# Linear attention, 32 heads: the second head's k on ScalarE's DMA queue, and a new order of the first two heads

## The chip, the core and the metric

The kernel runs on one core of a Trainium2 chip. The metric is the device time of one execution in microseconds (us). Work is spread over TensorE (PE; its weight loads are shown as PEld), VectorE (DVE), ScalarE (ACT) and GpSimd (POOL); SyncE (SP) issues the DMAs. Each of these runs its own list of instructions in order and waits on semaphores for the others.

## The reference

q, k and v are bf16, 1 x 32 heads x 2048 rows x 128 columns; the output has the same shape.

```python
def reference(q, k, v):
    phi_q = jnp.where(q > 0, q + 1, jnp.exp(q)) + 1e-6
    phi_k = jnp.where(k > 0, k + 1, jnp.exp(k)) + 1e-6
    kv = jnp.einsum("bhsd,bhse->bhde", phi_k, v)
    z = jnp.einsum("bhsd->bhd", phi_k)
    num = jnp.einsum("bhqd,bhde->bhqe", phi_q, kv)
    den = jnp.einsum("bhqd,bhd->bhq", phi_q, z)[..., None] + 1e-6
    return num / den
```

The kernel writes phi(x) as the sum of two parts, min(exp(x), 1) + 1e-6 and max(x, 0), and multiplies by each part in its own matmul. z comes out of the same matmuls as kv, as a column of ones beside v.

## The kernel before

A head is 16 tiles of 128 rows. Per head h, the operations are these. The number after the dot is a part of the head (halves, for the first head's k, v and q), and the line is that of the profile of before.

- SP, L324: ldk, ldq, ldv load the head's k, q and v, 512 KB each, into one of 7 buffers; L418: st stores the result.
- ACT, L336: ek = exp(k). L372: eq = exp of q transposed, read from PSUM. L378: rqa = relu of the first 8 tiles of q transposed. L362: kvs copies kv from PSUM to SBUF.
- DVE, L339: em finishes exp(k). L342: rkd = max(k, 0) for half the tiles. L374: emq finishes exp(q). L381: rqb = max(q, 0) for the tiles that rqa leaves. L403 and L410: r and f, reciprocal of the denominator and division.
- POOL, L350: v1 copies v beside the column of ones. L346: rkp = max(k, 0) for the other tiles.
- PE, L368: T transposes q into the PSUM tile xT. L357: kv, 32 matmuls for kv and z of the head, accumulated in one PSUM tile. L389, L394, L396: n, numerator and denominator. L315: w1, w2 and w0 are matmuls on the identity whose result nobody reads (4, 4 and 15 of them).

There is one xT and one kv tile in PSUM. So T of head h+1 waits for eq, rqa and rqb of head h, and kv of head h+1 waits for kvs of head h. ek and em write one of two buffers, which is free again when kv two heads earlier is through.

Nothing is scheduled at run time: for every engine the order is a list written out by hand (ORDER), and the program derives from it which semaphores each operation waits for. Before the change the lists begin like this:

```python
"PE":  w1 w2 T0.1 T0.0 w0 T1.0 kv0.0 kv0.1 kv1.0 kv1.1 n0.0 n0.1 T2.0 ...
"DVE": eps0 ones rkd0.0 v1ones1 v1ones0 eps2 rkd1.0 em0.0 rqb0.0 emq0.0 emq0.1 em0.1 em1.0 rqb1.0 ...
"ACT": ek0.0 ek0.1 eq0.1 eq0.0 rqa0 ek1.0 eq1.0 kvs0 ek2.0 rqa1 kvs1 ek3.0 eq2.0 ...
"POOL": ident0 ident v10.0 rkp0.0 v10.1 rkp1.0 v11.0 rkp2.0 ...
"SP":  ldk0.0 ldq0.0 ldk1.0 ldv0.0 ldq1.0 ldv1.0 ldk2.0 ...
```

From the third head on, the same round repeats. The loads run ahead of the work as far as the 7 buffers and the DMA queue allow.

Of the kernel before, what the change touches and what calls it, by code (L numbers as in the profile page):

```python
# [4 lines left out]
ACT = mybir.ActivationFunctionType  # L5
ALU = mybir.AluOpType
P = 128
EPS = 1e-6
ENGINES = ("PE", "DVE", "ACT", "POOL", "SP")
NH = 32  # L10
NI, NO, NE, NR, NV, NQ, NK = 7, 12, 2, 2, 2, 2, 2
WARM = (15, 4, 4)
HALVES = ((0, 8), (8, 16))
# [14 lines left out]
def q_parts(h):  # L28
    return HALVES if h == 0 else ((0, 8), (8, 12), (12, 16)) if h == NH - 1 else WHOLE

# [17 lines left out]
def na(h):  # L48
    return NA[h]


def groups(h):
    if h == NH - 1:
        return ((0, 2, 3, 0), (6, 2, 3, 2), (12, 2, 2, 4))
    return ((0, 4, 3, 0), (12, 2, 2, 4))


def st_parts(h):
    return ((0, 6), (6, 12), (12, 16)) if h == NH - 1 else WHOLE

# [10 lines left out]
def t_parts(h):  # L71
    return HALVES if h in (0, NH - 1) else WHOLE


def rqb_parts(h):
    if na(h) == 16:
        return ()
    if h == NH - 1:
        return tuple(p for p in q_parts(h) if p[0] >= na(h))
# [2 lines left out]

ORDER = {
    "PE": """
        w1 w2 T0.1 T0.0 w0 T1.0 kv0.0 kv0.1 kv1.0 kv1.1 n0.0 n0.1 T2.0 kv2.0 kv2.1 n1.0 T3.0 n1.1 kv3.0 kv3.1 n2.0
        T4.0 n2.1 kv4.0 kv4.1 n3.0 T5.0 n3.1 kv5.0 kv5.1 n4.0 T6.0 n4.1 kv6.0 kv6.1 n5.0 T7.0 n5.1 kv7.0 kv7.1 n6.0
        T8.0 n6.1 kv8.0 kv8.1 n7.0 T9.0 n7.1 kv9.0 kv9.1 n8.0 T10.0 n8.1 kv10.0 kv10.1 n9.0 T11.0 n9.1 kv11.0 kv11.1
        n10.0 T12.0 n10.1 kv12.0 kv12.1 n11.0 T13.0 n11.1 kv13.0 kv13.1 n12.0 T14.0 n12.1 kv14.0 kv14.1 n13.0 T15.0
# [5 lines left out]
        n30.0 n30.1 n31.0 n31.1 n31.2  # L94
    """,
    "DVE": """
        eps0 ones rkd0.0 v1ones1 v1ones0 eps2 rkd1.0 em0.0 rqb0.0 emq0.0 emq0.1 em0.1 em1.0 rqb1.0 rkd2.0 eps1
        emq1.0 rkd3.0 r0.0 em2.0 f0.0 em3.0 rqb2.0 r0.1 emq2.0 f0.1 r1.0 rkd4.0 f1.0 em4.0 rqb3.0 r1.1 rkd5.0 f1.1
        r2.0 emq3.0 f2.0 em5.0 rqb4.0 r2.1 rkd6.0 f2.1 r3.0 emq4.0 f3.0 em6.0 rqb5.0 r3.1 rkd7.0 f3.1 r4.0 emq5.0
        f4.0 em7.0 rqb6.0 r4.1 rkd8.0 f4.1 r5.0 emq6.0 f5.0 em8.0 rqb7.0 r5.1 rkd9.0 f5.1 r6.0 emq7.0 f6.0 em9.0  # L100
# [12 lines left out]
        emq31.0 r29.1 f29.1 r30.0 f30.0 r30.1 f30.1 emq31.2 r31.0 f31.0 r31.1 r31.2 f31.1 f31.2  # L113
    """,
    "ACT": """
        ek0.0 ek0.1 eq0.1 eq0.0 rqa0 ek1.0 eq1.0 kvs0 ek2.0 rqa1 kvs1 ek3.0 eq2.0 kvs2 rqa2 ek4.0 eq3.0 kvs3 rqa3
        ek5.0 eq4.0 kvs4 rqa4 ek6.0 eq5.0 kvs5 rqa5 ek7.0 eq6.0 kvs6 rqa6 ek8.0 eq7.0 kvs7 rqa7 ek9.0 eq8.0 kvs8
        rqa8 ek10.0 eq9.0 kvs9 rqa9 ek11.0 eq10.0 kvs10 rqa10 ek12.0 eq11.0 kvs11 rqa11 ek13.0 eq12.0 kvs12 rqa12
        ek14.0 eq13.0 kvs13 rqa13 ek15.0 eq14.0 kvs14 rqa14 ek16.0 eq15.0 kvs15 rqa15 ek17.0 eq16.0 kvs16 rqa16
# [10 lines left out]
        v128.0 rkp28.0 v129.0 rkp29.0 v130.0 rkp30.0 v131.0 rkp31.0  # L130
    """,
    "SP": """
        ldk0.0 ldq0.0 ldk1.0 ldv0.0 ldq1.0 ldv1.0 ldk2.0 ldk3.0 ldv2.0 ldq2.0 ldv3.0 ldq3.0 ldk4.0 ldv4.0 ldk5.0
        ldq4.0 ldv5.0 ldk6.0 ldq5.0 ldq6.0 ldv6.0 ldk7.0 ldq7.0 ldk8.0 st0.0 ldv7.0 ldv8.0 ldv9.0 ldk9.0 ldk10.0
        ldq8.0 ldk11.0 ldq9.0 st1.0 ldv10.0 ldq10.0 ldq11.0 ldk12.0 ldk13.0 ldv11.0 ldv12.0 ldq12.0 st2.0 ldv13.0
        ldk14.0 ldk15.0 ldv14.0 ldq13.0 ldq14.0 st3.0 ldq15.0 ldq16.0 ldk16.0 ldv15.0 ldq17.0 st4.0 ldv16.0 ldk17.0
# [19 lines left out]
class Program:  # L156
# [10 lines left out]
    def add(self, eng, key, fn, deps=(), dma=None, inc=True):  # L167
        assert key not in self.op, key
        self.op[key] = (eng, fn, tuple(deps), dma, inc)
# [71 lines left out]
def bass_standalone__linear_attn_elu__prompt_kernel(nc: bass.Bass, q: bass.AP, k: bass.AP, v: bass.AP, out: bass.AP):  # L241
    B, H, S, D = q.shape
    assert D == P and S == 16 * P and B * H == NH
    NT = S // P
# [6 lines left out]
    rows = lambda t, h: t[h].rearrange("(p j) d -> p j d", j=NT)  # L251

    with ExitStack() as es:
        names = [0]

        def alloc(make, shape, dt):
            names[0] += 1
            return es.enter_context(make(f"la_{names[0]}", shape, dt))
# [5 lines left out]
        sb = lambda shape, dt=bf16: alloc(nc.sbuf_tensor, shape, dt)  # L264
# [5 lines left out]
        rden_sb = sb([P, 2, NT], fp32)  # L270
        o_sb = sb([P, NO, NT, D])
        ident, ones, epsr = sb([P, P]), sb([P, P]), sb([P, 3])
        xT = alloc(nc.psum_tensor, [P, NT, P], bf16)
        o_ps = alloc(nc.psum_tensor, [P, 6 * 512], fp32)
        KV0 = 5 * 512 + 2 * NC
# [3 lines left out]
        add = pr.add  # L279
# [26 lines left out]
        add("DVE", "eps1", lambda g: g.memset(epsr[0:1, :], eb), ["eps0"])  # L306
        add("DVE", "eps2", lambda g: g.memset(epsr[32:33, :], ec), ["eps0"])
        add("DVE", "ones", lambda g: g.memset(ones[:], 1.0))
        for s in range(NV):
            add("DVE", f"v1ones{s}", lambda g, s=s: g.memset(v1_sb[:, s, :, D:D + 2], 1.0))  # L310

# [9 lines left out]
            warm(f"w{i}", n)  # L321

        def load(name, dst, src, h, i, t0, t1, last):
            add("SP", f"ld{name}{h}.{i}", lambda e: e.dma_start(dst[:, h % NI, t0:t1], rows(src, h)[:, t0:t1]),  # L324
                last, dma=f"{name}{h % NI}.{i}")

        def head(h):
            for i, (a, b) in enumerate(ld_parts(h)):
                load("k", k_sb, kf, h, i, a, b, freed(NI, h, ("ek", k_parts), ("rkd", rkd_parts), ("rkp", rkp_parts)))
            for i, (a, b) in enumerate(ld_parts(h)):  # L330
                load("q", q_sb, qf, h, i, a, b, freed(NI, h, ("T", t_parts)))
            for i, (a, b) in enumerate(ld_parts(h)):
                load("v", v_sb, vf, h, i, a, b, freed(NI, h, ("v1", v_parts)))
# [130 lines left out]
```

## Time and profile before

| | |
|---|---|
| median of 7 runs | 170.62 us (169.57 to 171.11) |
| the profiled execution | 170.46 us, of which span 169.1 us |
| mean granted TensorE clock | 0.995 |
| busy: PE, PEld, DVE, ACT, POOL | 158.5, 153.1, 154.2, 153.7, 85.3 us |
| DMA | 67.53 MB, mean 399 GB/s over the span |

The span is the time from the first to the last instruction of the profile, and the rest of the 170.46 us lies around it. Matmuls overlap, so the pitch of a group of matmuls (from its start to the start of the next group) says more than its busy time. A timeline row gives the start, the busy time, the engine and line, the operation with its tiles and how many instructions were merged; in brackets stands how long the engine had been idle and what ended that. Rows of one engine may overlap by some 0.1 us, since the next instruction starts before the last has written everything.

The lines in 40 slices show how full the engines are over the span:

```profile
DVE  1297799999999999999999999999999989999990
ACT  3999899999999999999999999999999999995800
POOL 1089546645566545655566554655456553535000
DMA  5999999999999999999999999999999999999984
```

### The profile page before, as it was taken

Reading aid. Unit: us, or ns where it says so; the run is one execution under the profiler, and the core shown is the slowest. Engines: PE = TensorE matmul, PEld = TensorE weight load, DVE = VectorE, ACT = ScalarE, POOL = GpSimd, SP = SyncE. Lnnn points to the kernel's source line nnn. Section 1 sums busy time; section 2 is a strip of 40 time slices with the busy share of each in tenths; the row PEclk is TensorE's granted clock in tenths of the full one; section 3 lists DMA queues with packets and bytes.
Section 4 is the critical chain, followed back from the end, with each engine's and each line's share of the span. In section 5 each row is a group of like instructions: output and inputs, shape, how many; then the busy total and the mean of one; then the engine's idle time right before and its main releaser. Section 6 shows DMA issues by size and latency. Waiting matters only on the chain.

```text
span 169.1 us, 6305 instructions
## 1 busy us (share of the span) xinstructions
PE 158.5 (94%) x2775; PEld 153.1 (91%) x2775; DVE 154.2 (91%) x267; ACT 153.7 (91%) x133; POOL 85.3 (50%) x71
## 2 busy tenths in 40 slices
PE   6997999999999999999999999999999999999750
PEld 2576999999999999999999999999999999999740
DVE  1297799999999999999999999999999989999990
ACT  3999899999999999999999999999999999995800
POOL 1089546645566545655566554655456553535000
PEclk9999999999999999999999999999999999999998
DMA  5999999999999999999999999999999999999984
GB/s 208 390 420 412 407 410 406 410 419 405 406 415 412 418 407 412 413 414 418 412 415 418 412 421 413 411 420 415 418 417 414 423 411 418 416 413 418 395 330 169
DMA packets 18748, 67.53 MB, mean 399 GB/s; under 512 B 2080, under 2 KB 2464, under 8 KB 18720
## 3 DMA queue, kind: packets, MB, share of 16 engines
q1 hardware_dynamic: 18720, 67.12, 98.5%
q8 instruction: 22, 0.36, 0.8%
q14 instruction: 6, 0.05, 0.1%
HBM read 50.33 MB, written 16.78 MB: 397 GB/s over the span
## 4 chain that ended last, share of the span: by engine, by line
ACT 46%; PE 17%; DVE 14%; DMA 13%; SPq 3%; POOL 3%; issue 1%; DVEq 0%
ACT la L372 18%; ACT la L336 17%; DMA la<-in_q_dram 9%; ACT la L378 9%; DVE la L410 8%; PE la L357 7%; DMA la<-in_v_dram 4%; PE la L394 4%; PE la L368 3%; PE la L396 3%; SPq L324 2%; ACT la L362 2%; DVE la L381 2%; DVE la L374 2%; POOL la L350 2%; POOL la L346 1%
## 5 line engine op out<-in xcount | busy, mean ns | idle before, releaser
L410 DVE TENSOR_TENSOR la<-la 128x1536 bf16<-128x1536 f32 (+2 forms) x65 | 77.6, 1195 | 0.3
L396 PE MATMUL la<-la 128*128 128x129 bf16 x512 | 67.7, 219 | 0.0
L394 PE MATMUL la<-la 128*128 128x129 bf16 x512 | 67.7, 218 | 0.0
L357 PE MATMUL la<-la 128*128 128x129 bf16 x1024 | 63.3, 220 | 1.2 <-POOL la L350 1.2
L350 POOL COPY la<-la 128x1024 int32<-128x1024 int32 (+1 forms) x33 | 40.3, 1221 | 46.3 <-DVE la L403 27.7
L372 ACT ACTIVATE la<-la 128x2048 bf16<-128x2048 bf16 (+2 forms) x35 | 60.4, 1730 | 3.5 <-PE la L396 2.0
L336 ACT ACTIVATE la<-la 128x2048 bf16<-128x2048 bf16 (+1 forms) x33 | 61.3, 1859 | 2.0 <-DMA la<-in_k_dram 2.0
L357 PEld LDWEIGHTS la<-la 128*128 128x128 bf16 x1024 | 59.3, 98 | 1.3 <-DVE la L381 1.3
L346 POOL TENSOR_SCALAR la<-la 128x1024 bf16<-128x1024 bf16 x32 | 44.5, 1390 | 22.9 <-DVE la L410 22.9
L396 PEld LDWEIGHTS la<-la 128*128 128x128 bf16 x512 | 49.3, 96 | 0.0
L394 PEld LDWEIGHTS la<-la 128*128 128x128 bf16 x512 | 47.0, 97 | 0.0
L368 PE MATMUL la<-la 128*128 128x128 bf16 x512 | 34.5, 222 | 0.7 <-DMA la<-in_q_dram 0.6
L389 PE MATMUL la<-la 128*128 128x3 bf16 (+1 forms) x192 | 32.4, 169 | 1.6 <-DVE la L410 1.6
L378 ACT ACTIVATE la<-la 128x1024 bf16<-128x1024 bf16 (+1 forms) x32 | 33.5, 1046 | 0.0
L368 PEld LDWEIGHTS la<-la 128*128 128x128 bf16 x512 | 29.8, 99 | 2.4 <-DMA la<-in_q_dram 1.2
L339 DVE TENSOR_SCALAR la<-la 128x2048 bf16<-128x2048 bf16 (+1 forms) x33 | 23.0, 700 | 0.0
L374 DVE TENSOR_SCALAR la<-la 128x2048 bf16<-128x2048 bf16 (+2 forms) x35 | 22.6, 650 | 0.0
L381 DVE TENSOR_SCALAR la<-la 128x1024 bf16<-128x1024 bf16 x31 | 21.0, 678 | 1.5 <-ACT la L372 1.2
L342 DVE TENSOR_SCALAR la<-la 128x1024 bf16<-128x1024 bf16 x32 | 14.9, 466 | 6.4 <-DMA la<-in_k_dram 6.0
L389 PEld LDWEIGHTS la<-la 128*128 128x128 bf16 x192 | 18.7, 97 | 2.1 <-DVE la L410 1.8
L403 DVE RECIPROCAL la<-la 128x12 f32<-128x12 f32 (+2 forms) x65 | 12.7, 197 | 1.9 <-PE la L396 1.0
L362 ACT ACTIVATE la<-la 128x129 bf16<-128x129 f32 x32 | 9.0, 282 | 0.5 <-PE la L357 0.5
(14 smaller groups left out, 11.8 us busy)
## 6 DMA issues: line engine op xcount, KB each, us to landing
la<-in_k_dram SPq DMA_DIRECT2D x32, 512.0 KB, 15.6
la<-in_q_dram SPq DMA_DIRECT2D x32, 512.0 KB, 15.6
la<-in_v_dram SPq DMA_DIRECT2D x32, 512.0 KB, 15.2
out_dram<-la SPq DMA_DIRECT2D x31, 512.0 KB, 15.5
out_dram<-la SPq DMA_DIRECT2D x2, 192.0 KB, 2.8
out_dram<-la SPq DMA_DIRECT2D x1, 128.0 KB, 3.9
```

Source lines behind the costliest of these rows:

```text
L336: add("ACT", f"ek{h}.{i}", lambda e, a=a, b=b: e.activation(em_sb[:, h % NE, a:b], k_sb[:, h % NI, a:b], ACT.Exp), over("ldk", h, ld_parts ...
L346: add("POOL", f"rkp{h}.{i}", lambda e, a=a, b=b: e.tensor_scalar(rk_sb[:, h % NR, a:b], k_sb[:, h % NI, a:b], BIG, 0.0, op0=ALU.min, op1=A ...
L350: add("POOL", f"v1{h}.{i}", lambda e, a=a, b=b: e.tensor_copy(v1_sb[:, h % NV, a:b, 0:D].bitcast(i32), v_sb[:, h % NI, a:b].bitcast(i32)), ...
L357: ins = e.matmul(kv_ps, lhsT=src[:, j], rhs=v1_sb[:, h % NV, j, 0:NC], start=(j + part == 0), stop=(j == NT - 1 and part == 1))
L368: ins = e.transpose(xT[:, j], q_sb[:, h % NI, j], ident[:])
L372: add("ACT", f"eq{h}.{i}", lambda e, a=a, b=b: e.activation(emq_sb[:, h % NQ, a:b], xT[:, a:b], ACT.Exp), over("T", h, t_parts, a, b) + fr ...
L374: add("DVE", f"emq{h}.{i}", lambda e, a=a, b=b: e.tensor_scalar(emq_sb[:, h % NQ, a:b], emq_sb[:, h % NQ, a:b], 1.0, EPS, op0=ALU.min, op1 ...
L378: add("ACT", f"rqa{h}", lambda e: e.activation(rq_sb[:, h % NQ, 0:n], xT[:, 0:n], ACT.Relu), over("T", h, t_parts, 0, n) + freed(NQ, h, (" ...
L389: e.matmul(_ap(o_ps[:, :], o + D, [[NC, m]]), lhsT=ones[:], rhs=epsr[:, 0:m], start=True, stop=False, skip_group_check=True)
L394: e.matmul(to, lhsT=emq_sb[:, h % NQ, t], rhs=kvs_sb[:, h % NK, 0:NC], start=False, stop=False, skip_group_check=True)
L396: ins = e.matmul(to, lhsT=rq_sb[:, h % NQ, t], rhs=kvs_sb[:, h % NK, 0:NC], start=False, stop=True, skip_group_check=True)
L410: return e.tensor_tensor(out=_ap(o_sb[:, :, :, :], first(o_sb[:, h % NO, t0, 0:1]) - first(o_sb[:, :, :, :]), [[m * D, nb], [D, m], [1, D] ...
```

## The change

Four edits, all in the first two heads:

- ldk1.0, the load of the second head's k, is taken out of SP's list and issued by ACT, on ACT's own DMA queue. In SP's list ldv0.0 now follows ldq0.0 directly.
- ACT's list begins with a new operation `exp`, an exponential of one column of the tile of ones into a small tile of its own, and then ldk1.0. `exp` waits for `ones` (DVE).
- On ACT ek1.0 moves ahead of eq0.1, eq0.0 and rqa0. On DVE em0.1 and em1.0 move ahead of rqb0.0, emq0.0 and emq0.1.
- On PE kv0.0 and kv0.1 move ahead of T1.0.

```diff
+BY_ACT = ('ldk1.0',)
...
     "PE": """
-        w1 w2 T0.1 T0.0 w0 T1.0 kv0.0 kv0.1 kv1.0 kv1.1 n0.0 n0.1 T2.0 kv2.0 kv2.1 n1.0 T3.0 n1.1 kv3.0 kv3.1 n2.0
+        w1 w2 T0.1 T0.0 w0 kv0.0 kv0.1 T1.0 kv1.0 kv1.1 n0.0 n0.1 T2.0 kv2.0 kv2.1 n1.0 T3.0 n1.1 kv3.0 kv3.1 n2.0
...
     "DVE": """
-        eps0 ones rkd0.0 v1ones1 v1ones0 eps2 rkd1.0 em0.0 rqb0.0 emq0.0 emq0.1 em0.1 em1.0 rqb1.0 rkd2.0 eps1
+        eps0 ones rkd0.0 v1ones1 v1ones0 eps2 rkd1.0 em0.0 em0.1 em1.0 rqb0.0 emq0.0 emq0.1 rqb1.0 rkd2.0 eps1
...
     "ACT": """
-        ek0.0 ek0.1 eq0.1 eq0.0 rqa0 ek1.0 eq1.0 kvs0 ek2.0 rqa1 kvs1 ek3.0 eq2.0 kvs2 rqa2 ek4.0 eq3.0 kvs3 rqa3
+        exp ldk1.0 ek0.0 ek0.1 ek1.0 eq0.1 eq0.0 rqa0 eq1.0 kvs0 ek2.0 rqa1 kvs1 ek3.0 eq2.0 kvs2 rqa2 ek4.0 eq3.0 kvs3 rqa3
...
     "SP": """
-        ldk0.0 ldq0.0 ldk1.0 ldv0.0 ldq1.0 ldv1.0 ldk2.0 ldk3.0 ldv2.0 ldq2.0 ldv3.0 ldq3.0 ldk4.0 ldv4.0 ldk5.0
+        ldk0.0 ldq0.0 ldv0.0 ldq1.0 ldv1.0 ldk2.0 ldk3.0 ldv2.0 ldq2.0 ldv3.0 ldq3.0 ldk4.0 ldv4.0 ldk5.0
...
+        first_sb = sb([P, 2])
...
+        add("ACT", "exp", lambda e: e.activation(first_sb[:, 0:1], ones[:, 0:1], ACT.Exp), ["ones"])
...
         def load(name, dst, src, h, i, t0, t1, last):
-            add("SP", f"ld{name}{h}.{i}", lambda e: e.dma_start(dst[:, h % NI, t0:t1], rows(src, h)[:, t0:t1]),
+            add("ACT" if f"ld{name}{h}.{i}" in BY_ACT else "SP", f"ld{name}{h}.{i}", lambda e: e.dma_start(dst[:, h % NI, t0:t1], rows(src, h)[:, t0:t1]),
                 last, dma=f"{name}{h % NI}.{i}")
```

## The prediction

> **What bounds the kernel now.** I read the page first: the engines' shares and the chain that ended last.
>
> ```profile
> PE 158.5 (94%) x2775; PEld 153.1 (91%) x2775; DVE 154.2 (91%) x267; ACT 153.7 (91%) x133; POOL 85.3 (50%) x71
> ACT 46%; PE 17%; DVE 14%; DMA 13%; SPq 3%; POOL 3%; issue 1%; DVEq 0%
> ```
>
> Three engines and the DMA stand near full, so the next view is busy time by stretch (columns: length, then PE, weight loads, DVE, ACT, POOL, the PE clock, the DMA share, GB/s).
>
> ```profile
> 20.00:40.00 20.00, 20.00 (x370) 19.94 (x368) 19.47 (x35) 20.00 (x19) 11.16 (x9) 1.00 1.03 409
> 80.00:100.00 20.00, 20.00 (x368) 19.83 (x366) 19.97 (x34) 20.00 (x18) 12.23 (x9) 1.00 1.02 415
> 120.00:140.00 20.00, 19.75 (x363) 19.53 (x361) 19.44 (x35) 19.70 (x18) 11.18 (x9) 1.00 1.03 416
> ```
>
> ACT is busy without a gap from 20 us on. The chain gives its round as eq 1.77, kvs 0.22, rqa 0.91, ek 1.80: 4.70 us a head. So a shift of ACT at 20 us goes through to the end, except where ACT later idles for something that does not shift, a load. The waits after 20 us and ACT's late rows show how much that is:
>
> ```profile
> PE la L368 <- DMA la<-in_q_dram: 0.2, 1, 0.2
> 137.16 1.88 ACT L372 ACTIVATE la<-la 128x2048 bf16<-128x2048 bf16 x1 [0.30 <-PE la L396]
> 155.96 1.51 ACT L372 ACTIVATE la<-la 128x512 bf16<-128x512 bf16 x2 [1.69 <-PE la L396]
> ```
>
> T27 waited 0.2 us for its q, and the exp behind it 0.30: at most 0.30 can be absorbed. The 1.69 belongs to PE's own order in the last head and moves with everything else. What the change is worth is therefore read in the first 20 us. Timelines of ACT, then PE, then DVE and POOL there (start, busy, engine and line; in brackets the idle time before and what ended it):
>
> ```profile
> 3.97 2.00 ACT L336 ACTIVATE la<-la 128x1024 bf16<-128x1024 bf16 x2 [1.96 <-DMA la<-in_k_dram]
> 6.35 1.94 ACT L372 ACTIVATE la<-la 128x1024 bf16<-128x1024 bf16 x2 [0.37 <-PE la L368]
> 9.07 1.92 ACT L336 ACTIVATE la<-la 128x2048 bf16<-128x2048 bf16 x1
> 11.35 1.88 ACT L372 ACTIVATE la<-la 128x2048 bf16<-128x2048 bf16 x1 [0.35 <-PE la L368]
> 13.16 0.28 ACT L362 ACTIVATE la<-la 128x129 bf16<-128x129 f32 x1
> 19.16 1.88 ACT L372 ACTIVATE la<-la 128x2048 bf16<-128x2048 bf16 x1 [0.78 <-PE la L368]
> ```
>
> ```profile
> 1.52 3.38 PE L315 MATMUL la<-la 128*128 128x480 bf16 x8 [1.52 <-POOL la L301]
> 5.28 1.87 PE L368 MATMUL la<-la 128*128 128x128 bf16 x16 [0.37 <-DMA la<-in_q_dram]
> 6.96 3.23 PE L315 MATMUL la<-la 128*128 128x480 bf16 x15
> 10.26 1.05 PE L368 MATMUL la<-la 128*128 128x128 bf16 x16
> 11.15 1.98 PE L357 MATMUL la<-la 128*128 128x129 bf16 x32
> 14.30 1.97 PE L357 MATMUL la<-la 128*128 128x129 bf16 x32 [1.17 <-POOL la L350]
> ```
>
> ```profile
> 7.64 0.43 DVE L342 TENSOR_SCALAR la<-la 128x1024 bf16<-128x1024 bf16 x1 [3.04 <-DMA la<-in_k_dram]
> 8.95 0.85 POOL L350 COPY la<-la 128x512 int32<-128x512 int32 x1 [7.48 <-DMA la<-in_v_dram]
> 9.77 1.21 POOL L346 TENSOR_SCALAR la<-la 128x1024 bf16<-128x1024 bf16 x1
> 10.93 0.80 POOL L350 COPY la<-la 128x512 int32<-128x512 int32 x1
> 13.12 1.03 POOL L350 COPY la<-la 128x1024 int32<-128x1024 int32 x1
> ```
>
> The names, in order. ACT: ek0, eq0, ek1, eq1, kvs0, eq2. PE: w1 w2, T0, the filler w0, T1, kv0, kv1. The four first transfers land at 3.97 (k0), 5.28 (q0), 7.64 (k1), 8.95 (v0). ACT's only idle between 3.97 and 19.16 is 0.37, 0.35, a 0.16 before kvs1, and 0.78: 1.66 us is all that a better prologue could win.
>
> **The change, part by part.**
>
> *ldk1 on ACT's queue.* One issue less on SP (0.42 us each), where v0 goes out at about 1.64 instead of 2.11. That wins nothing: issues run ahead of landings by 3.2 us at k0 and 6.8 at v0, so the transfers wait for the DMA engines. On ACT the issue takes as long (no row of ACT; SP's are 0.38 to 0.47), while ACT idles until 3.97. Cost nothing; without that idle, 0.4.
>
> When does k1 join? ACT's issue goes out between 0.74 (when SP's first does, if it need not wait for the engine) and 2.3 (table load until 2.01, and an exp of one column no longer than the 0.28 of kvs). A transfer's step is 1.31 us (3.97 to 5.28), so k0's service began by 2.66, at most 1.9 after its issue: k1 joins between 2.7, or less, and 4.2, just when q0's turn comes at 3.97. Before, q0 stood ahead of k1; now they share. The bounds for q0: 5.28, if it is still served first, and 7.64, the landing of the third transfer before, if it becomes third. Joining at 4.2 with equal shares would give 6.4, and the long third step (2.36 against 1.31) comes on top. I take 7.64, the row for "three transfers are through". v0 remains fourth, 8.95: the same four have to land by then.
>
> [...] No row of before shows two queues of loads.
>
> *`exp`.* One activation of a column, at most 0.28, in idle time before 3.97. It shifts no table load: that stands at 0.73 already. Nothing.
>
> *ek1 ahead of eq0.* ek1 (1.80) can follow ek0 as soon as k1 is there; eq0, rqa0 and rqb0 come later. Nothing is lost by that in itself: eq0 would start at 9 to 10, rqa0 end at 12.4 and T1, which needs them, is later still (below). If k0 shares with k1 too, ek0 slips by up to 1.3; the same cover hides it. On DVE, em0 and em1 ahead of rqb0 and emq0 keep the same instructions; rkd1 waits for a k1 that lands no later. Nothing.
>
> *kv0 ahead of T1 on PE.* This is the price. T1 no longer stands right behind w0. kv0.0 needs v10.0 and kv0.1 needs v10.1, POOL's copies of v0 (8.95 to 9.77, and 10.93 to 11.73). Behind T1 hangs eq1, and behind eq1 on ACT stands kvs0, which frees the one PSUM tile that kv1 writes: kv1 now waits for eq1 as well. And xT is one buffer, so eq1 cannot start from anything else.
>
> Sum with q0 at 7.64, by pitches of the rows: T0 at 7.65; w0 1.68 later (5.28 to 6.96) at 9.33; kv0 3.30 later (6.96 to 10.26) at 12.63, after v10.1 at 11.73; T1 after kv0's 1.81 (32 matmuls in the chain) at 14.44; eq1 1.09 later (10.26 to 11.35) at 15.53 instead of 11.35; kvs0 1.81 later at 17.34; kv1 after its 0.28 and a 0.03 handover at 17.65 instead of 14.30: **3.35 late**. From kv1 the order is the old one: eq2 starts 4.86 after kv1 (14.30 to 19.16), at 22.5, and ACT's own sequence (1.81 + 0.18 + 1.79 + 0.90 + 0.17 + 1.80 = 6.65 after eq1, 22.18) gets there sooner. ACT, DVE and PE leave the prologue 3.35 late, 0.30 is taken back at T27: +3.05. On the profiled execution (170.46, of which span 169.1) that is 173.5; the median of the runs lies 0.16 above it: **173.7**.
>
> *The filler's clock.* w1 and w2 ran 0.42 a matmul (3.38 / 8), w0 0.215 (3.23 / 15), on the same shape: TensorE's faster pace came at about 7 us, after an idle of only 0.37. Now PE may idle from 4.90 to 7.65. Bounds: 0 (w0 at 0.215) and 15 x 0.205 = 3.1 (all of w0 at 0.42). I take 0 in the sum, w0's own row being the nearest, and keep 3.1 for the range.
>
> [...]
>
> **Rivals.**
>
> *q0 is not held up.* k1 joins too late and lands third at 7.64. For it: the later bound of joining, 4.2. Against it: the earlier one, and that an equal share already costs q0. Then w0 ends at 10.26, kv0.0 runs, kv0.1 waits for v10.1 until 11.75, T1 at 12.66, eq1 at 13.75, kv1 at 15.87: +1.57, less 0.30: 171.9. If the long third step vanished too and v0 came 1.05 sooner, w0 would set kv0 (10.26), eq1 13.16, kv1 15.28: +0.98 less 0.30, 171.3.
>
> *The filler runs slow.* All of the 3.1 on top: 176.8; half of it 175.2. For it: the idle of 2.7 us where there was 0.37.
>
> *The shift is swallowed, no slower.* The DMA, at a share of 1.02 or more and with a 15.34 us queue for T27's q in the chain, sets the end, and the engines only wait less for loads: 170.6. It decides if engines on the path waited for loads after 20 us by at least the shift. The waits give 0.2 for PE and 0.30 for ACT; POOL's waits for v are longer, but POOL is half idle. A gain would need eq2 before 19.16, so kv1 before 14.30, so eq1 by 12.18; even with v0 in time w0 and kv0 put it at 13.16.
>
> **How the numbers follow.** Forecast 0.52, its own range 172.6 to 174.8 (q0 at 6.5 to 7.64, some of w0 slow). q0 not held up 0.22; slow filler 0.18; swallowed 0.05; something unforeseen 0.03. The range 171.7 to 175.6 leaves out the swallowed case, the cheapest of the first rival, and the worst of the slow filler. About 0.5%, 0.85 us, is what a measurement of this kernel tells from no change. Same: the swallowed case and the 171.3 corner, 0.08; faster 0.03; slower 0.89.
>
> **What would show it.** In the profile of the changed kernel T0 starts at 6.4 to 7.65 (5.28 if the first rival holds), w0 at 3.2 us in all (more if the filler is slow), T1 behind kv0 at about 14.4, eq1 near 15.5 with an ACT idle of 2 to 3 us before it, kv1 near 17.6 released by kvs0 and not by POOL, POOL's first copy still at about 8.95, and from there a 4.70 round as before. I am wrong if POOL's first copy starts near 6.5, if eq1 starts before 12.5, or if ACT shows idle time after 25 us that takes the shift back.

## The result, and the profile after

| | before | after |
|---|---|---|
| median | 170.43 us (31 runs, 169.57 to 171.28) | 172.52 us (12 runs, 171.68 to 175.16) |
| the profiled execution, and its span | 170.46, 169.1 us | 171.75, 170.2 us |

The ratio is 1.0142, with a 95% interval of 1.0114 to 1.0169; a ratio leaves out runs more than 1.5% above the fastest of their kernel, here the two longest of the twelve, and in the table of experiments below one run each of three kernels and four of twelve of the last. The kernel is slower, and 172.5 lies inside the range on record, 1.2 below the forecast. The profiled execution is among the fastest of the twelve, so the traces are compared first, and the scatter of the runs afterwards.

The first 20 us, in the same views as before: ACT (with ACT's own DMA issue), PE, then DVE and POOL. Lines of the changed kernel lie 3 higher: L339 is ek, L375 eq, L365 kvs, L371 T, L318 the filler, L360 kv, L353 v1.

```profile
1.07 0.40 ACTq L327 DMA_DIRECT2D la<-in_k_dram  x1
3.95 3.86 ACT L339 ACTIVATE la<-la 128x1024 bf16<-128x1024 bf16 x3 [1.72 <-DMA la<-in_k_dram]
7.71 1.92 ACT L375 ACTIVATE la<-la 128x1024 bf16<-128x1024 bf16 x2
14.67 1.88 ACT L375 ACTIVATE la<-la 128x2048 bf16<-128x2048 bf16 x1 [4.12 <-PE la L371]
21.65 1.88 ACT L375 ACTIVATE la<-la 128x2048 bf16<-128x2048 bf16 x1 [0.27 <-PE la L371]
```

```profile
6.56 1.89 PE L371 MATMUL la<-la 128*128 128x128 bf16 x16 [1.65 <-DMA la<-in_q_dram]
8.24 3.69 PE L318 MATMUL la<-la 128*128 128x480 bf16 x15
11.76 1.98 PE L360 MATMUL la<-la 128*128 128x129 bf16 x32
13.57 1.06 PE L371 MATMUL la<-la 128*128 128x128 bf16 x16
16.77 1.02 PE L360 MATMUL la<-la 128*128 128x129 bf16 x15 [2.14 <-ACT la L365]
```

```profile
5.90 0.43 DVE L345 TENSOR_SCALAR la<-la 128x1024 bf16<-128x1024 bf16 x1 [1.33 <-DMA la<-in_k_dram]
7.85 1.15 POOL L353 COPY la<-la 128x512 int32<-128x512 int32 x1 [6.39 <-DMA la<-in_v_dram]
```

ek0.0, ek0.1 and ek1 run without a gap (the x3 row), as the change means them to. Then ACT is idle for 4.12 us: eq1 waits for T1, T1 stands behind kv0, kv0 behind the filler, and T0 behind a q that lands third. kv1 starts at 16.77 instead of 14.30, released by kvs0 and no longer by POOL; eq2 is 2.49 late.

The end of both kernels: the two last divisions on DVE (L410 is L413 after), then SP's own wait for the stores (total, times, longest).

```profile
163.60 1.54 DVE L410 TENSOR_TENSOR la<-la 128x768 bf16<-128x768 f32 x2
SPq L435 <- DMA out_dram<-la: 3.2, 2, 2.2
```

```profile
166.49 1.55 DVE L413 TENSOR_TENSOR la<-la 128x768 bf16<-128x768 f32 x2
SPq L438 <- DMA out_dram<-la: 1.4, 2, 0.9
```

The work ends at 165.14 before and at 168.04 after, **2.9 later**. But the span ends 4.0 after the work before, and only 2.2 after it in the changed kernel. The tail gives 1.8 back, and the span is 1.1 longer.

### The profile page after: what moved, and what is told of

Read it like the earlier page. It is cut to its first block, busy times and chain, and to the rows that moved or that the text cites. A ratio compares the mean times of both kernels' runs of the same rounds, so it can differ in the third digit from the quotient of the medians.

```text
span 170.2 us, 6304 instructions
## 1 busy us (share of the span) xinstructions
PE 158.8 (93%) x2775; PEld 153.2 (90%) x2775; DVE 152.6 (90%) x267; ACT 153.6 (90%) x134; POOL 85.9 (50%) x71
## 4 chain that ended last, share of the span: by engine, by line
ACT 49%; DVE 29%; PE 14%; DMA 3%; issue 2%; SPq 0%; DVEq 0%
ACT la L375 20%; ACT la L339 18%; DVE la L413 14%; ACT la L381 9%; PE la L360 4%; DVE la L377 4%; DVE la L384 4%; PE la L371 3%; DMA la<-in_q_dram 3%; DVE la L342 3%; ACT la L365 2%; DVE la L406 2%; PE la L397 2%; PE la L318 2%; PE la L399 2%
## 5 line engine op out<-in xcount | busy, mean ns | idle before, releaser
L413 DVE TENSOR_TENSOR la<-la 128x1536 bf16<-128x1536 f32 (+2 forms) x65 | 77.6, 1195 | 0.3
L375 ACT ACTIVATE la<-la 128x2048 bf16<-128x2048 bf16 (+2 forms) x35 | 60.3, 1730 | 6.8 <-PE la L371 4.4
L360 PE MATMUL la<-la 128*128 128x129 bf16 x1024 | 63.3, 220 | 2.1 <-ACT la L365 2.1
L353 POOL COPY la<-la 128x1024 int32<-128x1024 int32 (+1 forms) x33 | 41.1, 1247 | 43.4 <-DVE la L406 37.0
L339 ACT ACTIVATE la<-la 128x2048 bf16<-128x2048 bf16 (+1 forms) x33 | 61.2, 1860 | 1.7 <-DMA la<-in_k_dram 1.7
L360 PEld LDWEIGHTS la<-la 128*128 128x128 bf16 x1024 | 59.3, 98 | 2.5 <-ACT la L365 2.3
L371 PE MATMUL la<-la 128*128 128x128 bf16 x512 | 34.6, 222 | 1.7 <-DMA la<-in_q_dram 1.7
L371 PEld LDWEIGHTS la<-la 128*128 128x128 bf16 x512 | 29.9, 99 | 2.8 <-DMA la<-in_q_dram 2.5
L384 DVE TENSOR_SCALAR la<-la 128x1024 bf16<-128x1024 bf16 x31 | 21.0, 678 | 6.3 <-ACT la L375 6.0
L342 DVE TENSOR_SCALAR la<-la 128x2048 bf16<-128x2048 bf16 (+1 forms) x33 | 21.8, 663 | 0.8 <-ACT la L339 0.8
L345 DVE TENSOR_SCALAR la<-la 128x1024 bf16<-128x1024 bf16 x32 | 14.3, 447 | 4.8 <-DMA la<-in_k_dram 4.2
L365 ACT ACTIVATE la<-la 128x129 bf16<-128x129 f32 x32 | 9.0, 283 | 0.3 <-PE la L360 0.3
```

The lines of the kernel that those rows point to most:

```text
L339: add("ACT", f"ek{h}.{i}", lambda e, a=a, b=b: e.activation(em_sb[:, h % NE, a:b], k_sb[:, h % NI, a:b], ACT.Exp), over("ldk", h, ld_parts ...
L353: add("POOL", f"v1{h}.{i}", lambda e, a=a, b=b: e.tensor_copy(v1_sb[:, h % NV, a:b, 0:D].bitcast(i32), v_sb[:, h % NI, a:b].bitcast(i32)), ...
L360: ins = e.matmul(kv_ps, lhsT=src[:, j], rhs=v1_sb[:, h % NV, j, 0:NC], start=(j + part == 0), stop=(j == NT - 1 and part == 1))
L371: ins = e.transpose(xT[:, j], q_sb[:, h % NI, j], ident[:])
L375: add("ACT", f"eq{h}.{i}", lambda e, a=a, b=b: e.activation(emq_sb[:, h % NQ, a:b], xT[:, a:b], ACT.Exp), over("T", h, t_parts, a, b) + fr ...
L413: return e.tensor_tensor(out=_ap(o_sb[:, :, :, :], first(o_sb[:, h % NO, t0, 0:1]) - first(o_sb[:, :, :, :]), [[m * D, nb], [D, m], [1, D] ...
```

## The experiments

Five questions were put. Is it the order on PE (A) or the late q (B) that costs? Is the queue what makes the new orders bearable (C)? Where does the tail's 1.8 come from: was the kernel before held at its end by the DMA queue (D), or is its end that of the compute chain, with 0.3 of slack (E)? Is the filler on the path (F)? And what makes the runs scatter: TensorE's granted clock (G, H)? All profiled executions, in us:

| kernel | eq2 starts | last division ends | span | from there to the end | median | ratio to before, 95% |
|---|---|---|---|---|---|---|
| before | 19.16 | 165.14 | 169.1 | 4.0 | 170.43 | |
| after | 21.65 | 168.04 | 170.2 | 2.2 | 172.52 | 1.0114 to 1.0169 |
| T1 put back | 20.20 | 165.75 | 168.2 | 2.4 | 169.72 | 0.9961 to 1.0000 |
| k1 back on SP | 21.04 | 167.40 | 169.9 | 2.5 | 171.11 | 1.0009 to 1.0095 |
| queue alone | 20.79 | 166.36 | 168.4 | 2.0 | 169.72 | 0.9969 to 1.0021 |
| ACT and DVE order alone | 21.53 | 167.89 | 171.0 | 3.1 | 172.43 | 1.0051 to 1.0156 |
| before, filler 23 | 19.88 | 165.70 | 169.1 | 3.4 | 170.30 | 0.9979 to 1.0023 |
| before, filler 31 | 20.66 | 166.22 | 168.7 | 2.5 | 170.77 | 0.9996 to 1.0041 |
| before, two loads cut | 18.73 | 164.29 | 166.7 | 2.4 | 168.56 | 0.9867 to 0.9940 |
| after, two loads cut | 22.03 | 168.41 | 170.8 | 2.4 | 173.19 | 1.0118 to 1.0205 |
| after, filler 5 | 21.63 | 168.11 | 170.1 | 2.0 | 170.68 | 0.9985 to 1.0055 |
| after, filler ahead of T0 | 22.16 | 168.52 | 170.5 | 2.0 | 170.26 | 0.9993 to 1.0072 |
| T1 put back, fillers moved | 19.01 | 165.30 | 168.3 | 3.0 | 169.64 | 0.9951 to 0.9988 |
| after, gap behind T1 filled | 22.55 | 168.93 | 171.1 | 2.2 | 171.89 | 0.9976 to 1.0061 |

The ratio is to runs of before on the same chip (medians 169.83 to 170.44), which allows for the chip; the median counts all runs. The profiled execution of the last three "after" kernels is one of their slower runs.

One thing in the table is a step, not a slope. In the seven kernels whose eq2 starts at 21.04 or later, the way from there to the end of the last division takes 146.4 to 146.5 us; in six of the others it takes 145.5 to 146.0 (T1 put back with fillers moved: 146.3). In those seven and in no other, PE waits 0.65 us for a division on DVE between 150 and 152 us, as in the changed kernel at 151.07. What makes that division late was not tried.

**T1 put back ahead of kv0**, the rest as changed.

```diff
-        w1 w2 T0.1 T0.0 w0 kv0.0 kv0.1 T1.0 kv1.0
+        w1 w2 T0.1 T0.0 w0 T1.0 kv0.0 kv0.1 kv1.0
```

> The changed kernel with T1.0 put back ahead of kv0.0 and kv0.1 on PE; the DMA queue and the ACT and DVE orders stay as changed. Theory A (the loss is kv0 standing ahead of T1, so that eq1 and kvs0 wait for it): w0 ends at 11.76 as in the changed kernel, T1 follows at once, eq1 starts at 12.85 instead of 14.67, kv1 at about 15.0 instead of 16.77, only 0.7 later than in the kernel before; the time falls from 172.5 to between 170.5 and 171.2. Theory B (the loss is the q that lands third, and the order on PE costs nothing): eq1 and kv1 stay within 0.3 of 14.67 and 16.77, and the time stays at 172.5.

```profile
13.17 1.88 ACT L375 ACTIVATE la<-la 128x2048 bf16<-128x2048 bf16 x1 [2.54 <-PE la L371]
15.32 1.87 PE L360 MATMUL la<-la 128*128 128x129 bf16 x30 [0.38 <-ACT la L365]
```

eq1 is 1.5 earlier than in the changed kernel, kv1 1.45, and the time is 169.72, lower than the range of A: the whole loss is gone, though q still lands third (T0 at 6.60) and the work still ends 0.6 later than before. A holds, B falls. That not even the remaining 0.6 costs anything speaks for D.

**k1 back on SP's queue**, all new orders kept.

```diff
-BY_ACT = ('ldk1.0',)
+BY_ACT = ()
...
-        exp ldk1.0 ek0.0
+        exp ek0.0
...
-        ldk0.0 ldq0.0 ldv0.0
+        ldk0.0 ldq0.0 ldk1.0 ldv0.0
```

> The changed kernel with the second head's k issued by SP in its old place; the orders on PE, ACT and DVE stay as changed. Theory A (the order on PE costs by itself, the late q adds to it): T0 is back at 5.28, w0 ends near 10.3, kv0.1 waits for POOL's copy or follows w0, eq1 starts at 13.2 to 13.8, kv1 at 15.3 to 15.9, and the time is 170.9 to 171.9. Theory B (the loss is the late q alone): kv1 is back at 14.3 and the time at 170.4. Theory C (the queue is what makes the new orders bearable, since ek1 would hold up eq0 until k1 has landed): eq1 at 14.7 or later, time 172.5 or more.

171.11 with a ratio of 1.0052: A again. T0 is back at 5.40, eq1 starts at 14.05 and kv1 at 16.16, some 0.3 beyond A's figures: the second half of kv0 began only at 12.05 (v0 landed at 9.28, and POOL's second copy of it ended at 11.91). B (170.4) and C (172.5 or more) fall: the orders cost without the late q too, but 0.9% less than with it.

**The queue alone**, all orders as before.

```diff
-        exp ldk1.0 ek0.0 ek0.1 ek1.0 eq0.1 eq0.0 rqa0 eq1.0
+        exp ldk1.0 ek0.0 ek0.1 eq0.1 eq0.0 rqa0 ek1.0 eq1.0
...
(DVE and PE as in the kernel before)
```

> The kernel before with only the new DMA queue: the exp of one column and ldk1.0 at the head of ACT's list, all orders of PE, ACT and DVE as before. Both theories: T0 at about 6.6, its q being third to land, w0 until 11.8. Theory A: T1 follows at 11.8, eq1 at 12.9, kv1 at 15.0 (0.7 late), time 170.5 to 171.2, the same as with T1 put back. Theory B (the late q is the loss): kv1 at 16.5 or later and 172 or more.

No difference from before, though T0 started at 7.01 and the work ended 1.2 later. kv1 came at 15.93, 0.9 later than A said, and the time lies below A's range; B falls. The busy time by stretch (the third number from the right is the PE clock) has the reason:

```profile
8.00:11.20 3.20, 3.20 (x11) 1.22 (x9) 2.25 (x4) 3.20 (x4) 2.89 (x4) 0.50 1.02 417
```

In this execution TensorE's granted clock was 0.50 for 3.2 us, after PE had sat idle for 2.30 before T0, and the filler took 4.79 instead of 3.23. The tail was 2.0 instead of 4.0: the lateness was swallowed there.

**The order on ACT and DVE alone**, k1 on SP and T1 first.

```diff
 (DVE; against the kernel before)
-        rkd1.0 em0.0 rqb0.0 emq0.0 emq0.1 em0.1 em1.0 rqb1.0
+        rkd1.0 em0.0 em0.1 em1.0 rqb0.0 emq0.0 emq0.1 rqb1.0
 (ACT)
-        ek0.0 ek0.1 eq0.1 eq0.0 rqa0 ek1.0 eq1.0
+        exp ek0.0 ek0.1 ek1.0 eq0.1 eq0.0 rqa0 eq1.0
```

> The kernel before with only ACT's and DVE's new order (ek1 ahead of eq0, em0.1 and em1 ahead of rqb0; the exp of one column leads ACT's list); k1 on SP's queue, T1 ahead of kv0 as before. ek1 has to wait for k1, which lands third. Theory A: with k1 at 7.64, ek1 7.64 to 9.44, eq0 until 11.3, rqa0 until 12.2, T1 at 12.25, eq1 at 13.35, kv1 at 15.5 (1.2 late), time 170.8 to 171.6; with k1 at 6.4 all of it is hidden and the time is 170.4. A rival by which the order of ACT and DVE is the main loss: kv1 at 16.5 or later, time 172 or more.

It costs 1.0104, where the queue alone cost nothing (PE's order alone, on the kernel before, was not run). The time and kv1 (16.64) are those of the rival, but not by the order's own work:

```profile
11.87 1.05 PE L371 MATMUL la<-la 128*128 128x128 bf16 x16 [2.04 <-ACT la L381]
12.76 3.51 PE L360 MATMUL la<-la 128*128 128x129 bf16 x32
```

```profile
12.90:16.30 3.40, 3.37 (x33) 3.10 (x30) 1.33 (x2) 1.88 (x1) 0.36 (x1) 0.50 1.02 408
```

T1 waited for rqa0 until 11.87, near A's figure, and eq1 began at 12.96, even earlier. But PE had been idle for 2.04, the granted clock fell to 0.50, and kv0 took 3.51 instead of 1.98. Five of the six runs were over 172 at a mean clock of 0.986 to 0.988; the sixth had 0.997 and 170.32. Two things stay open. The tail here is 3.1, against 2.2 in the changed kernel, whose work ends as late. And T1 stands first here: with k1 on SP, T1 first costs 1.0104 and T1 behind kv0 1.0052 (the intervals overlap), so without the late q the place of kv0 shows no price of its own.

**More filler in the kernel before**: a pure delay of the prologue.

```diff
-WARM = (15, 4, 4)
+WARM = (23, 4, 4)
```

> The kernel before with the filler w0 at 23 matmuls instead of 15: 8 x 0.215 = 1.7 us more ahead of T1, everything else as before. T1 at 12.0, eq1 at 13.1, kv1 at about 15.2, 0.9 late. Theory D (before, the end is set by the DMA queue: the last stores wait for transfers ahead of them, so a shift of the work by up to some 1.8 us costs little): time within 0.2 of before, and the last store lands 2.1 to 3.2 after the last division instead of 3.9. Theory E (ACT's chain sets the end and only the 0.3 at T27 is absorbed): 0.6 slower.

```diff
-WARM = (15, 4, 4)
+WARM = (31, 4, 4)
```

> The kernel before with w0 at 31 matmuls: 3.4 us more ahead of T1. eq1 at 14.8, kv1 at 16.9, 2.6 late, about as late as in the changed kernel but with no second DMA queue and no change of order. Theory D: the last division 2.3 to 2.9 later, the time 0.7 to 1.4 slower than before, the last store landing some 2.1 after the last division. Theory E: 2.3 slower.

eq2 moved by 0.72 and 1.50, less than meant, since in both executions the quicker pace came sooner (T0 took 1.07 instead of 1.87) and ate part of the delay. The ratio is 1.0001 and 1.0019. So 0.7 us of delay is free, and of 1.5 us some 0.3 (0.0019 of 170.4) is left. E wanted 0.6 and 2.3 for the delays as planned, 0.4 and 1.2 for those that came about (less its 0.3). The interval of the first run reaches 0.4, that of the second only 0.7, so E falls by the second. D stands, though its 0.7 to 1.4, meant for a longer delay, was missed too.

**Two loads cut**, in the kernel before and in the changed one.

```diff
         def load(name, dst, src, h, i, t0, t1, last):
+            if name == "v" and h in (18, 22):
+                t1 = t0 + 2
```

> The kernel before with two of the 96 loads cut: v of heads 18 and 22 is loaded for 2 of its 16 tiles only (the rest of the buffer keeps an older head's v, so these two heads' outputs are not the reference's). That takes 0.92 MB, some 2.3 us at 412 GB/s, from the DMA engines and nothing from the compute engines. Theory D: the time falls by 1.2 to 2.1, the last division moves by 0.3 at most, and the last store lands about 2.1 after it instead of 3.9. Theory E: within 0.4 of before.

> The changed kernel with the same two loads cut to 2 of 16 tiles (heads 18 and 22 are not the reference's). Theory D (in the changed kernel the compute chain sets the end, since the last store already lands 2.1 after the last division): within 0.3 of the changed kernel, 171.7 to 172.6. Rival (the DMA sets the end of both kernels): 1.2 to 2.1 faster than the changed kernel.

This decides it. With 0.92 MB less of transfers and no less compute, the kernel before falls by 0.97% (1.7 us), the changed one shows no gain (ratio to before 1.0162, against 1.0142; the rival's 1.2 us less would be 1.007). It has six runs only: three at 172.2 to 172.5, as D said, and three at 173.9 to 174.2 with a mean clock of 0.978 to 0.986. In the profile of before with the cut:

```profile
162.74 1.55 DVE L412 TENSOR_TENSOR la<-la 128x768 bf16<-128x768 f32 x2
SPq L437 <- DMA out_dram<-la: 1.6, 2, 0.9
```

the last division starts 0.86 earlier (half of it a prologue that came 0.43 earlier in this execution; D had allowed 0.3), and the tail is 2.4 instead of 4.0. The kernel before is held at its end by the DMA queue, the changed one by its work.

**A shorter filler in the changed kernel.**

```diff
-WARM = (15, 4, 4)
+WARM = (5, 4, 4)
```

> The changed kernel with the filler w0 at 5 matmuls instead of 15. Theory F (since q lands third, the filler behind T0 lies on the path to kv0, T1 and eq1): w0 ends near 9.8, kv0.1 waits for POOL's copy of v until 10.7, T1 at 11.7, eq1 at 12.7 to 13.2 instead of 14.67, kv1 near 15, and the time falls to 169.6 to 170.6. Rival (the filler is hidden behind POOL and eq0): eq1 and the time stay within 0.4 of the changed kernel, 172.5.

```profile
13.06 1.88 ACT L375 ACTIVATE la<-la 128x2048 bf16<-128x2048 bf16 x1 [2.35 <-PE la L371]
```

eq1 is 1.6 earlier: the filler is on the path (F). But the runs split in two: six at 169.6 to 169.9, six at 171.5 to 171.7. The profiled one is of the upper six, and in it eq2 is no earlier than in the changed kernel: ACT waits 1.85 us for T2 (0.27 there), and T2 comes behind the 2.14 us in which PE waits for kvs0. That the clock fell in between is the author's estimate, from this wait and the mean clock of 0.990. The mean clocks of the two groups overlap (0.989 to 0.999 and 0.987 to 1.000), so the mean clock does not sort them.

**Filler ahead of T0 in the changed kernel**, where PE waited for q.

```diff
-WARM = (15, 4, 4)
+WARM = (15, 4, 8)
```

> The changed kernel with four more filler matmuls ahead of T0 (w2 of 8 instead of 4), which keep PE busy from 4.9 until about 6.5, while it waits for q. Theory G (the idle time before T0 delays TensorE's faster pace, and that makes T0 and the first of w0 slow, in some executions more than in the profiled one): T0 takes 1.1 instead of 1.9, w0 is at 0.215 a matmul throughout, eq1 starts 0.7 to 1.2 earlier, and the times from 173.5 up are gone: all runs within 171.0 to 172.0. Rival (the pace has nothing to do with it, the spread of the changed kernel's times comes from elsewhere): eq1 within 0.3 of 14.67 and the same spread, 171.7 to 175.

T0 takes 1.07 instead of 1.89, the filler 0.21 a matmul, eq1 starts 1.1 earlier: the first half of G holds. Of the second, the times from 173.5 up are gone, but no run lies within 171.0 to 172.0: seven runs lie at 169.7 to 170.6 (mean clock 0.996 to 1.000), five at 172.0 to 172.2 (0.986 to 0.989). One of the five was profiled:

```profile
12.00:16.50 4.50, 2.36 (x43) 2.19 (x41) 1.02 (x4) 2.93 (x3) 3.02 (x3) 1.00 1.03 409
16.50:20.00 3.50, 3.50 (x39) 3.50 (x37) 1.05 (x4) 3.19 (x4) 0.00 (x0) 0.51 1.03 408
```

The clock falls after the *other* idle time, the 2.14 us in which PE waits for kvs0 behind T1, and kv1 and the first n run slowly (39 matmuls in those 3.50 us, 76 in the next 4.00). That price was not in the prediction. Why the other seven are some 2 us below the changed kernel's runs at full clock (171.7 to 172.6), for an eq1 that is 1.1 earlier, no profile shows; the step of the table is a candidate.

**That gap filled**, in the changed kernel.

```diff
-        w0 kv0.0 kv0.1 T1.0 kv1.0
+        w0 kv0.0 kv0.1 T1.0 w3 kv1.0
...
-WARM = (15, 4, 4)
+WARM = (15, 4, 4, 8)
```

> The changed kernel with one edit: 8 filler matmuls (1.7 us at 0.215) between T1 and kv1, where PE waited 2.14 us for kvs0. The work is no earlier by it: eq1 at 14.7, kv1 at 16.8. Theory H (the upper group of the changed kernel's times, 173.8 to 175.2 at a mean granted clock of 0.986 to 0.989 in five of twelve runs, is this idle time making the granted clock drop for 3.4 us): that group is gone, all times 171.5 to 172.8, and the median falls to 171.7 to 172.4. Rival (the upper group has another cause, such as the two DMA queues): about as many runs above 173.5 as before.

H holds in part. The runs above 173.5 are gone, no run has a clock under 0.99 any more, and the median of 171.89 is where H put it. But that is still 1.1% above before on the same chip (170.10), where the changed kernel was 1.2% above. The runs reach from 169.5 to 173.1, beyond H's range on both sides, and the two at 173.1 have a mean clock of 1.000: something other than a drop of the clock scatters them too. In the profiled one, at 172.44 and a mean clock of 0.990, the slow matmuls stand elsewhere, behind the 2.39 us of idle time before T0: the first five of the filler take 2.20 us (0.44 each), and the whole filler 4.64 instead of 3.69:

```profile
7.04 1.34 PE L371 MATMUL la<-la 128*128 128x128 bf16 x16 [2.39 <-DMA la<-in_q_dram]
```

So slow matmuls followed both gaps, each in some executions; the granted clock itself was read at 0.50 behind the gap before T0 with the queue alone, and at 0.51 behind the other one with the filler ahead of T0. What the runs at 169.6 did otherwise no profile shows.

**T1 put back, fillers moved** ahead of T0: the new queue and ACT's order without what held them up.

```diff
-        w1 w2 T0.1 T0.0 w0 kv0.0 kv0.1 T1.0 kv1.0
+        w1 w2 T0.1 T0.0 w0 T1.0 kv0.0 kv0.1 kv1.0
...
-WARM = (15, 4, 4)
+WARM = (8, 4, 8)
```

> The changed kernel with T1.0 back ahead of kv0, four more fillers ahead of T0 (w2 of 8) and 8 instead of 15 behind it: the prologue with the new queue and without what was found to hold it up. T1 at about 10.6, eq1 at 11.7, kv1 at 13.8, 0.5 ahead of the kernel before. Theory D (the DMA queue sets the end of the kernel before): no more than 0.4 faster than T1 put back alone, 169.3 to 169.7, the last store 2.6 or more behind the last division. Theory E (the compute chain sets the end): 169.0 or less.

169.64, 0.9969 of before (0.9951 to 0.9988): the one version whose interval lies wholly below before, by 0.3%, in D's range. eq1 started at 11.98 and eq2 at 19.01, no earlier than in the kernel before to speak of. Its lowest run equals that of before on the same chip (169.33); what is gone is the upper part of the spread (169.83 at most, against 171.1). Its tail of 3.0 fits a floor set by the DMA queue, but since the work ended no earlier than before (165.30 against 165.14), this run does not tell D from E.

## Why the prediction was right or wrong

*Direction and mechanism: right, and shown.* In the changed kernel kv0 ahead of T1 is the price: put back alone, it takes the whole loss away. It is not the only way: with kv0 still first, the shorter filler (0.9985 to 1.0055) and the filler ahead of T0 (0.9993 to 1.0072) take most of it away too. The late q, the filler, kv0 and T1 stand in one chain, and some 1.2 us of lateness are free. PE's order alone, on the kernel before, was not run. T1 behind kv0, eq1 with a long idle time before it, and kv1 released by kvs0 are in the profile as written.

*When k1 joins: right.* ACT issued at 1.07, beside its table load, without waiting for it. k1 landed at 5.90, q0 third at 6.56: inside the 5.28 to 7.64 given, and far from the 7.64 taken. The long third step (2.36) did not come back. **This term was mis-sized by 1.08**, and the sum for kv1 by 0.88 (17.65 against 16.77). The slower filler took back 0.22 (pitch 3.52 instead of 3.30): the clock's bounds held, near the low end. v0 landed at 7.85, not at 8.95, by the same short step, but w0 and not POOL set kv0, so nothing came of it. That eq2 would follow at the old distance from kv1 held (4.88 against 4.86).

*That q0 would be held up: right.* No row of before shows two queues of loads, so that q0 and k1 would share was the author's estimate. In the changed kernel k1 was there at 5.90 and q0 at 6.56, where before q0 was there at 5.28 and k1 at 7.64.

*What absorbs the shift: wrong.* The sum gave back 0.30 at T27. That wait is gone in the changed kernel, but another one stands in its place:

```profile
154.16 1.88 ACT L375 ACTIVATE la<-la 128x2048 bf16<-128x2048 bf16 x1 [0.71 <-PE la L399]
```

The shift of 2.49 at eq2 had grown to 2.9 at the last division: it is the step of the table, in which PE waits for a division on DVE and ACT behind it. What gave time back was the tail, 1.8 us, which the sum had left out. It looked for slack only in waits of the compute engines inside the span; the rival of the swallowed shift had the right mechanism, but priced it all or nothing at 0.05. The two traces add up: 3.35 predicted, less 0.88, and 0.4 more on the way, less 1.8 in the tail, is 1.1.

*The scatter: not foreseen.* The clock was considered for the filler alone. Its larger price is the drop that may follow PE's 2.14 us of idle time behind T1 (3.5 us at 0.51 with the filler ahead of T0), which the prediction's own sum contained (eq1 at 15.53, kv1 at 17.65) without anyone asking what the clock does meanwhile. Runs of the changed kernel at a clock of 0.985 to 0.989 are mostly 173.8 to 175.2 (one is 172.48), the others 171.7 to 172.6. None of the slower ones was profiled: that this drop is theirs is argued from the filler ahead of T0, where a profile shows it, and from the gap filled, where they are gone. It is not the whole scatter. The mean clock, for one, does not tell when the quicker pace first began: the record reads 1.00 even from 1.5 to 4.9 us, where w1 and w2 run at 0.42 a matmul. That the median of 172.5 lies inside the range, 1.2 below the forecast, is partly luck: the sum was too dear by the late q (0.88) and the tail (1.8), too cheap by the step (0.4) and the scatter.

## What to carry to other kernels

Before a shift is carried through to the end, look at what the end itself waits for: if the last stores queue behind others, a delay of the work is free up to that queue (here some 1.2 us). A gain should then be worth nothing, which no run here tests. On one engine's list, the operation that feeds the longest chain goes first: kv0 was ready when T1 was, and its place cost T1 the whole of its run. Count idle time on TensorE twice, once as time and once for the clock that may drop after it: in three of these executions 2.04 to 2.30 us of it were followed by 3.2 to 3.5 us at 0.50 or 0.51, while in the profile of the changed kernel 2.14 us were not.

## What the runs showed of the hardware

- With k1 on ACT's queue the third and fourth load landed sooner. The third of the first transfers (as the first engine that waited for it shows) was there at 6.56 to 7.04 in the eight kernels with k1 on ACT's queue (mean 6.8), and at 7.12 to 8.36 in the six with all loads on SP's (mean 7.75), before and after included; the fourth, v0, at 7.85 to 8.33 against 8.45 to 9.65. Why was not tried.
- An idle time of 2.04 to 2.30 us on PE was followed, in three of the profiled executions, by 3.2 to 3.5 us at a granted clock of 0.50 or 0.51: 8.00 to 11.20 with the queue alone (idle for 2.30), 12.90 to 16.30 with the order on ACT and DVE alone (2.04), 16.50 to 20.00 with the filler ahead of T0 (2.14). In the profiled execution of the changed kernel, where PE is idle for the same 2.14 us behind T1, the clock stays at 1.00:

```profile
12.62:16.03 3.41, 2.01 (x36) 1.83 (x33) 0.00 (x0) 1.36 (x1) 2.31 (x3) 1.00 1.03 410
16.03:19.45 3.42, 2.68 (x49) 2.68 (x50) 2.06 (x5) 3.42 (x5) 0.00 (x0) 1.00 1.03 406
```

  What decides between the two was not shown. One such drop takes 0.010 off a mean clock, as an estimate (3.4 us at 0.50 in a span of 170); the kernel before, in whose profile PE's longest idle times after 1.52 are 1.17 us and, in the last head, 1.60, is above 0.990 in 96 of its 97 runs that list one (the other has 0.989). In the profiles of before and of the changed kernel the granted clock falls to 0.50 once, at 167.4 and 169.6 us, where no matmul is left (the last start at 163.25 and 166.13).
- A DMA issued by ACT started at 1.07 while a table load ran on ACT from 0.73 to 2.01, and ahead of the `exp` that stands before it in ACT's list (2.02): the issue did not wait for the engine.
